# Attention with part of its exponentials on VectorE: one shared factor for the shifted terms, GpSimd adds of two of them, eight key tiles instead of five, and order constants by block

## The chip, the cores and the metric

The kernel runs on one core of one Trainium2 chip. The metric is device time in microseconds of one execution, and lower is better. The engines that matter are TensorE (PE in the profile, with its weight loads as PEld), ScalarE (ACT), VectorE (DVE) and GpSimd (POOL). Each has its own queue of instructions and meets the others only through semaphores. SP is the queue that starts most of the DMAs.

## The reference, cut to what matters

The layer normalises the input, runs an attention of 16 heads of width 28 and, beside it, a feed-forward layer with GELU. The output is x + attention * silu(feed-forward).

```python
xn = _layernorm(x)                                  # 2048 x 448
qkv = (xn @ wqkv).reshape(1, 2048, 3, 16, 28) ...   # q, k, v by head
scores = einsum("bhqd,bhkd->bhqk", q, k) * 28**-0.5
p = softmax(scores)                                 # 16 heads x 2048 x 2048
s = einsum("bhqk,bhkd->bhqd", p, v) ... @ wo        # 2048 x 448
h = gelu(xn @ w1 + b1)                              # 2048 x 1792
g = silu(h @ w2 + b2)
out = x + s * g
```

The softmax has 16 x 2048 x 2048 = 67 million exponentials, and they are most of the work of the element-wise engines.

## The kernel before, in words

**Tiling.** The heads go in four groups of four (G = 4), the queries in four chunks of 512 (C = 4). One group and one chunk make a block, so there are NBLK = 16 blocks. A block has 16 key tiles of 128 keys times 4 heads: 64 score tiles of 128 keys x 512 queries, numbered m, MTOT = 1024 in all. In the last block the same tiles are cut by query columns (`pieces`). Scores are computed with keys on the partitions, so a tile of exponentials goes straight into the product with V, which is accumulated in one PSUM bank (`acc`) for the block. A row of V that is constant gives the softmax sum.

**Two ways for an exponential.** Most tiles go through ACT: `p_scores` computes two tiles (or three, where a third PSUM bank is free: `third`, allowed by block by the tuple `R3`) in one row-tiled PE task, `p_exps` evaluates the exponential of the two or three banks in one ACT instruction (line 1407), and the results lie in one of the P slots until `t_pv` (line 1762) multiplies them with V, four heads side by side in four column strips of PE. The others, called late here and in the code, go through DVE in groups of four tiles (one key tile, four heads). Their scores ride in the free rows of the score tasks (`attach`) or go alone (`p_solo`). `p_apass` (line 1625) turns each score bank into a 16-bit integer by one multiply and add; read as bf16, this is a piecewise linear power of two. `p_expq` (line 1684) makes two more copies of the four tiles by adding an integer of the tuple `SH` to it, which shifts the piecewise curve; the weighted sum of the three curves is close to the exponential. The weights (`VC`) are not applied to the tiles but to V: `p_vs` (line 1695) has GpSimd write a scaled copy of the V tile for either shifted term, and the product with V then takes three passes for a late tile, one with V and two with the scaled copies, where an ACT tile takes one.

**Which tiles are late.** `p_late` asks block by block for NQ[b] groups; `pick` takes the next key tile of the list VT = (15, 14, 13, 12, 11), if it lies at least QDIST tiles ahead of the scores, so that a block can have five groups at most (two in the last block, where it takes a pair of key tiles). It goes on only if fewer than ND4 groups are unfinished, the queue of late scores is shorter than LQ and three buffers (units) of 128 x 2048 are free. A unit is held until the product with V has read it.

**What sets the order.** Nothing is scheduled by hand. The builder runs a planner: every step is a generator that offers tasks with an engine, buffers read and written, an expected duration and a priority; `run` keeps a clock for each engine, always takes the task that could start first (within EPS the one with the better priority), writes its instruction into that engine's queue and the waits before it. So the constants (durations, priorities, distances, NQ) decide the order in each queue, and the chip then runs these fixed queues. `port=True` marks tasks on DVE and GpSimd that the planner keeps from overlapping: the shifts of `p_expq`, the squares of q, the multiply at the end of a block. Projections, the feed-forward products, the normalisation by the softmax sum (`p_epi`: SP DMAs, a power on GpSimd of line 1826, a multiply on GpSimd of line 1835) and the output are further generators with due times (`planned`) in units of m. At m = 584 (GM), in block 9, ACT changes to the GELU and back.

Of the kernel before, what the change touches and what calls it, by code (L numbers as in the profile page):

```python
# [8 lines left out]
ALU = mybir.AluOpType  # L9
ET = mybir.EngineType  # L10

PE, ACT, DVE, POOL, SP = ET.PE, ET.Activation, ET.DVE, ET.Pool, 5

S = 2048
D = 448
# [3 lines left out]
G = 4  # L19
C = 4  # L20
# [6 lines left out]
NBLK = G * C  # L27
MTOT = NBLK * T * 4

GM = 584  # L30
NQ = (3, 14, 13, 13, 17, 3, 14, 8, 16, 1, 21, 18, 14, 14, 18, 21)
QLEAD, QDIST = 60, 20
JMAX, DQ, LQ, ND4, LU = 4, 8, 2, 4, 16
PV0, PVC, MP = 12, 3, 0.124
SLACK = 0.413
URG = 10
SP, AHEAD = 5, 101
R3 = (1, 1, 1, 2, 1, 1, 1, 1, 1, 2, 1, 0, 1, 0, 0, 1)
DUE, UR, M0, M2 = 13, 0.922, 59, 978
VT = (15, 14, 13, 12, 11)  # L40
SM_SCALE = DH ** -0.5
LOG2E = 1.4426950408889634
SH = (0, 42, 85)
VC = (1.0, 0.79296875, 0.63671875)
EXP_LC = 1.6446
NS = 5
EXP_OFF = 64.0 / (LOG2E * SM_SCALE)
LN_EPS = 1e-5
KNORM = 2.5
# [9 lines left out]
SBT = [(f // FT, f % FT) for f in range(F0)]  # L59
SEM, OWN = 0.07, 0.03  # L60
SWITCH = 0.1
JOINT = 0.15
EPS = 0.1
PVN = 2
OVERLAP = 0.083
# [28 lines left out]
class _Kernel:  # L94
# [23 lines left out]
    def sb(self, name, shape, dtype=dt.bfloat16):  # L118
        return self.es.enter_context(self.nc.sbuf_tensor(name, shape, dtype))
# [106 lines left out]
        return min(range(len(self.banks)), key=lambda i: (max(self.free_at(i), self.tE[PE]), self.banks[i][1] in third), default=None)  # L226

    def settle(self):
        again = True
        while again:  # L230
            again = False
            for p in sorted(self.procs, key=lambda p: (-1 if p[4]() else p[0], p[1])):
                op = p[3]
                if isinstance(op, _Task):
                    continue
                if op[0] == "until" and op[1]():
                    self.advance(p)
                    again = True

    def run(self):  # L240
        idle = 0
# [50 lines left out]

    def due(self, *key):
        m = self.plan[key]
        return lambda: 5 if self.in_gelu() else 1.1 if self.next_m > m else SP

    def planned(self):
        K = self
# [46 lines left out]
    def alloc(self):  # L345
# [28 lines left out]
        self.ones = sb("ones", [128, 1], bf)  # L374
        self.csq = sb("csq", [128, G], bf)
        self.colK = sb("colK", [128, G], f32)
        self.vs = sb("vs", [128, 2, NS, 2, 4, 32], bf)
        self.coff = sb("coff", [128, 1], f32)
        self.b2b = self.wv[:, 0, 0:D]
        self.st6 = sb("st6", [128, T, 6], f32)  # L380
# [105 lines left out]
    def schedule(self):  # L486
# [33 lines left out]
        K.late_left = [0] * (NBLK + 3)  # L520
        K.vt = [list(VT) for g in range(G)]
        K.late_on = False
        assert all(len(x) <= NS for x in K.vt)
        K.PB, K.PPREV, K.plast = {}, {}, {}
        K.free_u = []
        K.a_left = {}
        K.h3_free = False
        K.pend_q = []
        K.copying = False
        K.ln2e = 0  # L530
        K.late_blk = 0
        K.banks += [(K.ring[:, b, :], K.b_ring[b]) for b in (3, 2)]
# [561 lines left out]

    def p_q(self, g, c):
        K = self
        bank, tok = yield ("bank", lambda: K.pe_free() and K.ready(K.b_xnT[c] + [K.b_wqk[0][g], K.b_colK, K.b_kT[0][3]]) and ((g, c) == (0, 1) or K.boot()), 1.5 if g == 0 else K.due("kq", g, c))
        K.pe_wait += 1
        for k in range(KT):
            yield K.t_proj(0, g, c, bank, tok, k, 1.5 if g == 0 else K.due("kq", g, c))  # L1100
        K.pe_wait -= 1
        qb = K.qT[:, g, c * 512:(c + 1) * 512]
        qr = _Buf()
        yield _Task(DVE, lambda eng: eng.tensor_copy(qb, bank), [tok], [qr], 0.7, 0.0, 2)  # L1104
        K.banks.append((bank, tok))
        yield ("until", lambda: len(K.qsqs) > 0 if g == 0 else (K.qn_done >= g - 1 and (g > 1 or K.q0_done == 3)))
        i = K.qsqs.pop(0) if g == 0 else c
        qs, tq = K.qsq[:, i, :], K.b_qsq[i]
        if g:
            yield _Task(POOL, lambda eng: eng.tensor_tensor(qs, qb, qb, ALU.mult), [qr], [tq], 1.1, 0.05, 2, port=True)  # L1110
        else:
            yield _Task(DVE, lambda eng: eng.tensor_tensor(qs, qb, qb, ALU.mult), [qr], [tq], 0.43, 0.0, 2, port=True)
        if g:
            K.qn[g].append(qr)
            return
        bank2, tok2 = yield ("bank", lambda: K.ready([tq]), 1.5)
        yield _Task(PE, lambda eng: eng.matmul(bank2, K.bsel[:, :], qs, start=True, stop=True),
                    [tq, K.b_bsel], [tok2], 0.216, 0.17, 1.5 if g == 0 else 4)
        K.qsqs.append(i)
        yield _Task(DVE, lambda eng: eng.scalar_tensor_tensor(qb, bank2, K.colK[:, g:g + 1], qb, op0=ALU.add,  # L1120
                                                              op1=ALU.add), [tok2, K.b_colK, qr], [qr, K.b_qT[g][c]], 0.75, 0.0, 2)
        K.banks.append((bank2, tok2))
        K.q0_done += 1

# [242 lines left out]
    def p_scores(self):  # L1367
        K = self
        u = 0
        while K.next_m < MTOT:  # L1370
            yield ("until", lambda: K.exp_u >= u - 2)
            if K.next_m >= MTOT:
                break
            if K.gu is not None and u == K.gu + 1:
                yield ("until", lambda: K.dir_read == ND)
            b0 = 4 * (u % 2)
            n = 2
            ms = []
            while len(ms) < n and K.next_m < MTOT:
                ms.append(K.next_m)  # L1380
                K.step()
            if K.gu is None and ms[-1] >= GM:
                K.gu = u
            at = {m: K.ring[:, b0 + k, :] for k, m in enumerate(ms)}
            toks = [K.b_ring[b0 + k] for k in range(len(ms))]
            K.pend = p = {"task": K.t_score(ms, at, toks, 1), "ms": ms, "at": at, "toks": toks, "rs": [], "b0": b0}
            yield p["task"]
            K.pend = None
            for (m0, u0, m), x in p["rs"]:
                K.spawn(K.p_apass(u0, m0, m - m0, *x), m0)  # L1390
            K.sc_u = u
            u += 1
# [99 lines left out]

    def pick(self, b):
        K = self
        for t in VT:
            m0 = 64 * b + (4 * t if b < NBLK - 1 else 2 * t - 2)
            if m0 % 4 or m0 in K.late or (b == NBLK - 1 and t - 1 not in VT):
                continue
            if m0 < K.next_m + QDIST:
                return None  # L1500
            K.late |= set(range(m0, m0 + 4))
            K.late_left[b] += 1
            K.nq += 1
            return m0
        return None
# [162 lines left out]
    def p_expq(self, m0, u):  # L1668
        K = self
        b = K.sub_of(m0)  # L1670
        yield ("until", lambda: K.ln2e == 0 and K.a_left[m0] == 0 and K.unit_of(b, 2 if not any(K.sub_of(x) < b for x in K.pend_q) else 4) is not None)
        K.ln2e = 1
        K.need -= 1
        K.pend_q.remove(m0)
        us = [u]
        for _ in range(2):
            v = K.unit_of(b)
            K.free_u.remove(v)
            us.append(v)
        u16 = dt.uint16  # L1680
        bT = K.b_U[u]
        for i in (1, 2):
            W, T, bW = *K.pair(us[i], u), K.b_U[us[i]]
            yield _Task(DVE, lambda eng, W=W, T=T, i=i: eng.tensor_scalar(W.bitcast(u16), T.bitcast(u16), float(SH[i]), None, op0=ALU.add),
                        bT, bW, 0.69, 0.0, 4, port=True)
        K.ln2e = 0
        K.late_ready.append((m0, tuple(us)))

    def p_vs(self, g):
        K = self  # L1690
        yield ("until", lambda: all(K.b_v[1 if g else 0][t].tw is not None for t in K.vt[g]) and (g < 2 or K.E_done >= C * (g - 2) + C - 1))
        for i, t in enumerate(K.vt[g]):
            for v in (1, 2):
                dst, src = K.vs[:, g % 2, i, v - 1, :, :], K.vaug[:, t, 4 * g:4 * g + 4, :]
                yield _Task(POOL, lambda eng, dst=dst, src=src, v=v: eng.tensor_scalar(dst, src, VC[v], 1.0, op0=ALU.mult, op1=ALU.mult),  # L1695
                            [K.b_v[1 if g else 0][t], K.b_vpad, K.b_vpad0], [K.b_vs[g % 2][i]], 0.36, 0.05, 2, port=True)

    def p_pv(self):
        K = self
# [4 lines left out]
        for q in range(0, MTOT // 4, 2):  # L1704
# [2 lines left out]
            b = first  # L1707
            mine = lambda: [x for x in K.late_ready if K.sub_of(x[0]) == b]
            go = lambda: K.exp_m >= ms[-1] and K.E_done >= first - 1
            low = lambda: q % 16 > 0 and K.E_done >= first - 1 and len(K.free_u) < LU and any(K.ready(K.b_U[x[1][-1]]) for x in mine())  # L1710
            while not go():
                yield ("until", lambda: go() or low())
                if not go():
# [1 line left out]
            while end and len(mine()) < K.late_left[b]:  # L1715
                yield ("until", lambda: len(mine()) == K.late_left[b] or (len(K.free_u) < LU and len(mine()) > 0))
                if len(mine()) < K.late_left[b]:
                    yield from self.pv_task(q, mine()[:1], [])
            late = [x for x in K.late_ready if K.sub_of(x[0]) == b and (end or K.ready(K.b_U[x[1][-1]]))]
            yield from self.pv_task(q, late, ms)  # L1720
            for m in ms:
                K.pv_done[m] = True
# [5 lines left out]
    def pv_task(self, q, late, ms):  # L1728
# [4 lines left out]
        K.late_left[b] -= len(late)  # L1733
        src = [(m,) + K.p_slot(m) + (0,) for m in ms if m not in K.late]
        for m0, us in late:
            for v, u in enumerate(us):
                src += [(m0 + k, K.part(u, k), K.b_U[u][k], v) for k in range(4)]
        for i in range(0, len(src), 4 * PVN):
            yield self.t_pv(q, src[i:i + 4 * PVN])
        for _, us in late:  # L1740
            K.free_u += us

    def t_pv(self, q, src):
        K = self
# [2 lines left out]
        for kk in range(4):  # L1747
            for m, ap, tok, v in src:
# [7 lines left out]
                K.pv_begun.add((K.sub_of(m), j))  # L1756

                i = K.vt[g].index(t) if v else 0
                w = K.vs[:, g % 2, i, v - 1, j, :] if v else K.vaug[:, t, 4 * g + j, :]

                def f(eng, j=j, q0=q0, nq=nq, col=col, ap=ap, first=first, w=w, t=t):
                    return eng.matmul(K.acc[32 * j:32 * j + 32, q0:q0 + nq], w,  # L1762
# [176 lines left out]
```

## Time and profile before

| | |
|---|---|
| median of 3 runs | 426.99 us (426.97 to 427.0) |
| profiled execution, its own time | 426.28 us |
| its span, first to last instruction | 424.0 us |
| ACT busy | 404.2 us in 414 instructions |
| PE busy | 402.6 us |
| DVE busy | 339.1 us in 585 instructions |
| GpSimd busy | 146.6 us in 159 instructions |
| first exponential starts | 14.0 us |

The span of the profiled execution is 2.3 us shorter than its own time, and that time 0.7 us shorter than the median. In the profile an instruction's record lasts from its start until its result is written, so records of one engine in a row overlap a little, and "busy" counts the overlap once. A PE that is busy by the records also counts the changes between its tilings, because the modelled end of a matmul reaches over them.

### The profile page before, as it was taken

The numbers are of one execution on the slowest core, as the hardware profiler recorded it, in microseconds if no ns is written. First come the engines' busy times: TensorE is split into PE (matmuls) and PEld (weight loads), VectorE is DVE, ScalarE is ACT, GpSimd is POOL, SyncE is SP. The second block draws the span as 40 slices with busy tenths as digits, with TensorE's granted clock in tenths as the row PEclk, the third lists the DMA queues.
The fourth block names the chain that finished last, engine by engine and source line by source line (L and its number), as shares of the span: only waits on it lengthen the run. The fifth ranks groups of instructions, "written<-read, shape, count | busy, mean of one in ns | idle before, by whom it ended". The sixth has DMA issues, their size and how long they took to land.

```text
span 424.0 us, 9666 instructions
## 1 busy us (share of the span) xinstructions
PE 402.6 (95%) x3708; PEld 136.8 (32%) x3735; DVE 339.1 (80%) x585; ACT 404.2 (95%) x414; POOL 146.6 (35%) x159
## 2 busy tenths in 40 slices
PE   6999999999999999999999999999999999999993
PEld 4443223332222222222223433332232223223551
DVE  7969999999698899996782132187999998999675
ACT  5899999999999999999999999999999999999990
POOL 6583032316351413222223210075083217421512
PEclk9999999999999999999999999999999999999999
DMA  8801010101010100000500100001000000002335
GB/s 265 305 2 39 2 27 2 28 2 36 6 26 2 27 2 23 6 3 27 152 27 5 24 1 2 2 2 29 2 26 2 10 20 21 7 3 57 60 72 88
DMA packets 15368, 15.30 MB, mean 36 GB/s; under 512 B 7037, under 2 KB 12393, under 8 KB 15274
## 3 DMA queue, kind: packets, MB, share of 16 engines
q1 hardware_dynamic: 14170, 12.61, 10.5%
q0 software_dynamic: 864, 1.38, 2.6%
q8 instruction: 30, 0.49, 0.5%
q10 hardware_dynamic: 288, 0.69, 0.4%
q14 instruction: 16, 0.13, 0.1%
HBM read 12.60 MB, written 3.40 MB: 38 GB/s over the span
## 4 chain that ended last, share of the span: by engine, by line
PE 59%; ACT 17%; issue 10%; DVE 7%; POOL 5%; POOLq 0%; ACTq 0%; DVEq 0%
PE ring L1354 18%; PE acc L1762 14%; ACT P L1407 10%; PE ring L1216 7%; ACT h L1407 7%; PE ring L1285 3%; PE misc L862 3%; PE ring L862 2%; PE misc L1285 2%; PE misc L1216 2%; POOL rc L1826 1%; PE acc L1004 1%; PE misc L1155 1%; PE misc L1845 1%; POOL h L1306 1%
## 5 line engine op out<-in xcount | busy, mean ns | idle before, releaser
L1407 ACT ACTIVATE P<-ring 128x1024 bf16<-128x1024 f32 (+1 forms) x248 | 260.7, 1171 | 2.4 <-PE ring L1354 1.8
L1354 PE MATMUL ring<-qT,kT 32*128 32x512 bf16 (+2 forms) x1072 | 143.7, 358 | 5.6 <-ACT h L1407 1.2
L1407 ACT ACTIVATE h<-ring 128x1024 bf16<-128x1024 f32 (+1 forms) x80 | 85.9, 1177 | 0.0
L1354 PEld LDWEIGHTS ring<-qT,kT 32*128 32x128 bf16 x1072 | 38.5, 91 | 139.9 <-ACT P L1407 78.4
L1826 POOL TENSOR_TENSOR rc<-rs,mone 128x16 f32<-128x16 bf16 x15 | 44.5, 2966 | 88.9 <-DMA rs<-sums 88.9
L1762 PE MATMUL acc<-P,vaug 128*32 128x512 bf16 (+2 forms) x638 | 52.6, 352 | 0.3 <-ACT P L1407 0.2
L1216 PE MATMUL ring<-xnT,w 128*128 128x512 bf16 x156 | 41.9, 382 | 1.0 <-issue 1.0
L1407 ACT ACTIVATE xnT<-ring 128x1024 bf16<-128x1024 f32 (+1 forms) x33 | 35.0, 1117 | 0.4 <-PE ring L1354 0.3
L1625 DVE TENSOR_SCALAR x_sb<-ring 128x512 uint16<-128x512 f32 x48 | 32.5, 685 | 3.5 <-PE ring L1354 3.3
L1835 POOL TENSOR_TENSOR qT<-x_sb,E_sb 128x512 bf16<-128x512 f32 x15 | 18.8, 1255 | 47.3 <-DMA x_sb<-recs 37.6
L1110 POOL TENSOR_TENSOR qsq<-qT 128x512 bf16<-128x512 bf16 x12 | 12.8, 1070 | 56.7 <-DVE qT L1104 40.5
L1285 PE MATMUL ring<-w,h 128*128 128x448 bf16 x126 | 30.2, 355 | 0.3 <-DVE qT L1104 0.3
L1354 PE MATMUL misc<-qT,kT 32*128 32x512 bf16 (+1 forms) x80 | 29.6, 376 | 0.0
L1625 DVE TENSOR_SCALAR h<-ring 128x512 uint16<-128x512 f32 x37 | 25.2, 686 | 2.1 <-PE ring L1354 1.2
L1762 PE MATMUL acc<-h,vaug 128*32 128x512 bf16 x220 | 26.2, 384 | 0.0
L1306 POOL TENSOR_TENSOR h<-w 128x448 bf16<-128x448 bf16 x12 | 13.6, 1134 | 35.3 <-ACT w L1301 34.7
L1285 PE MATMUL misc<-w,h 128*128 128x448 bf16 x98 | 25.1, 356 | 0.5 <-DVE w L1291 0.4
L1216 PEld LDWEIGHTS ring<-xnT,w 128*128 128x128 bf16 x164 | 13.8, 97 | 21.3 <-issue 6.5
L1695 POOL TENSOR_SCALAR vs<-vaug 128x128 bf16<-128x128 bf16 x40 | 14.5, 362 | 17.3 <-PE acc L1762 9.3
L1762 PEld LDWEIGHTS acc<-P,vaug 128*32 128x32 bf16 x638 | 13.8, 95 | 15.2 <-issue 11.4
L1291 DVE TENSOR_TENSOR w<-misc,wv 128x448 bf16<-128x448 f32 x7 | 4.3, 620 | 17.2 <-PE misc L1285 17.2
L1216 PE MATMUL misc<-xnT,w 128*128 128x512 bf16 x56 | 17.2, 384 | 0.5 <-issue 0.5
(251 smaller groups left out, 653.2 us busy)
## 6 DMA issues: line engine op xcount, KB each, us to landing
x_sb<-recs SPq DMA_DIRECT2D x60, 64.0 KB, 2.0
w<-in_B_w_dram SPq DMA_DIRECT2D x1, 1568.0 KB, 7.3
w<-in_B_w_dram SPq DMA_DIRECT2D x1, 1344.0 KB, 8.2
out_dram<-in_A_x_dram SPq DMA_DIRECT2D x3, 448.0 KB, 10.7
out_dram<-h POOLq DMA_DIRECT2D x6, 224.0 KB, 4.0
x_sb<-in_A_x_dram SPq DMA_DIRECT2D x2, 448.0 KB, 5.3
h<-in_A_wqkv_dram SPq DMA_DIRECT2D x3, 168.0 KB, 5.1
x_sb<-in_A_x_dram ACTq DMA_DIRECT2D x1, 448.0 KB, 4.3
```

What stands on the lines that cost most here:

```text
L862: return eng.matmul(bank, w[:, k, g * 128:(g + 1) * 128], K.xnT[:, k, c * 512:(c + 1) * 512], start=(k == 0), stop=(k == KT - 1))
L1110: yield _Task(POOL, lambda eng: eng.tensor_tensor(qs, qb, qb, ALU.mult), [qr], [tq], 1.1, 0.05, 2, port=True)
L1216: return eng.matmul(bank, K.w1[:, k, ft * 128:(ft + 1) * 128], K.xnT[:, k, c * 512:(c + 1) * 512], start=(k == 0), stop=(k == KT - 1))
L1285: ins = eng.matmul(ps, hv[:, ft, t * 128:(t + 1) * 128], K.w2[:, ft, :], start=(ft == 0), stop=(ft == FT - 1))
L1306: yield _Task(POOL, lambda eng, o=o, t=t: eng.tensor_tensor(o, sg[:, t, :], fb[:, t, :], ALU.mult), [K.b_sig[c % 2], K.b_fsb[c % 2]], [K.b ...
L1354: return eng.matmul(dst, K.kT[32 * j:32 * j + 32, g, t * 128:(t + 1) * 128], K.qT[32 * j:32 * j + 32, g, c * 512 + q0:c * 512 + q0 + nq], ...
L1407: return eng.activation(reg[:, i0:i0 + n, :], K.ring[:, b0:b0 + n, :], ACTF.Exp, scale=SM_SCALE)
L1625: yield _Task(DVE, lambda eng: eng.tensor_scalar(K.part(u, k).bitcast(dt.uint16), K.like(u, bank), SM_SCALE * LOG2E * 128.0, (127.0 - EXP_ ...
L1695: yield _Task(POOL, lambda eng, dst=dst, src=src, v=v: eng.tensor_scalar(dst, src, VC[v], 1.0, op0=ALU.mult, op1=ALU.mult), [K.b_v[1 if g ...
L1762: return eng.matmul(K.acc[32 * j:32 * j + 32, q0:q0 + nq], w, ap[:, col:col + nq] if len(ap.shape) == 2 else ap[:, col // 128:(col + nq) / ...
L1826: yield _Task(POOL, lambda eng: eng.tensor_tensor(K.rc[:, :], K.rs[:, :], K.mone[:, 0:1].to_broadcast([128, 16]), ALU.pow), [K.b_srs, K.b_ ...
L1835: yield _Task(POOL, lambda eng: eng.tensor_tensor(dst, K.rb, E, ALU.mult), [K.b_rb, tE], [K.b_onT[g][c]], 1.15, 0.05, 1, port=True)
```

## The change: what it does

- **One factor.** `SH` and the constant of the first pass change, and both shifted terms now have the same weight, VC = 0.6875. There is one scaled copy of V a key tile instead of two.
- **Adds on GpSimd.** With one weight the two shifted terms can be added before the product. In blocks whose constant MG is 1, when the scores are more than GE tiles from the end of the group's block and GpSimd's planned queue ends within GQ us, `p_expq` has GpSimd add the third term into the second, in four adds of 128 x 512; one unit becomes free at once and the product takes two passes instead of three. By the change's own words that is a third of the groups.
- **Eight key tiles.** VT has eight entries, and the cap of a block is eight groups (four in the last). NQ changes with it, and `R3`.
- **Constants by block.** The table BP has a row of 18 constants for each block; `tune` puts a row into force when the scores enter the block.
- **Smaller edits.** The first projection of q of the second chunk gets better priorities (Q1, QP); `settle` goes over the waiting generators in another order; readiness of a group looks at all its buffers; the variable SP that stood for two things is split.

```diff
+BPN = ('MG', 'GQ', 'GE', 'EPS', 'PV0', 'PVC', 'MP', 'ND4', 'LU', 'JOINT', 'LQ', 'JMAX', 'DQ', 'URG', 'SLACK', 'UR', 'QLEAD', 'QDIST')
+BP = (
+    (1, 4.0, 12, 0.1, 12, 3, 0.124, 4, 16, 0.15, 2, 4, 8, 8, 0.413, 0.922, -1, 20),
+    (0, 4.0, 12, 0.1, 12, 3, 0.124, 4, 16, 0.116, 2, 4, 8, 8, 0.413, 0.922, 60, 20),
...
+    (1, 4.0, 12, 0.1, 12, 3, 0.124, 4, 16, 0.15, 2, 4, 8, 10, 0.413, 0.922, 60, 20),
+)
-NQ = (3, 14, 13, 13, 17, 3, 14, 8, 16, 1, 21, 18, 14, 14, 18, 21)
+NQ = (3, 13, 13, 13, 14, 5, 15, 8, 16, 4, 16, 16, 12, 14, 15, 16)
...
-R3 = (1, 1, 1, 2, 1, 1, 1, 1, 1, 2, 1, 0, 1, 0, 0, 1)
+MG, GQ, GE = 1, 4.0, 12
+GP, MP4 = 4.2, 1
+R3 = (1, 0, 1, 2, 1, 1, 0, 2, 1, 0, 1, 0, 0, 1, 0, 1)
-VT = (15, 14, 13, 12, 11)
+VT = (15, 14, 13, 12, 11, 10, 9, 8)
-SH = (0, 42, 85)
-VC = (1.0, 0.79296875, 0.63671875)
-EXP_LC = 1.6446
-NS = 5
+SH = (0, 40, 82)
+VC = 0.6875
+EXP_LC = 1.60626
+NS = 8
...
     def settle(self):
-        again = True
-        while again:
-            again = False
-            for p in sorted(self.procs, key=lambda p: (-1 if p[4]() else p[0], p[1])):
...
+        while True:
+            on = [p for p in self.procs if not isinstance(p[3], _Task) and p[3][0] == "until" and p[3][1]()]
+            if not on:
+                return
+            for p in sorted(on, key=lambda p: (-1 if p[4]() else p[0], p[1])):
+                if p[3][1]():
                     self.advance(p)
...
+    def tune(self, b):
+        if BP:
+            globals().update(zip(BPN, BP[b]))
...
     def p_q(self, g, c):
+        dp = Q1 if (g, c) == (0, 1) else 2
+        pp = QP if (g, c) == (0, 1) else 1.5
...
     def p_scores(self):
...
+            if K.next_m // 64 != K.blk:
+                K.blk = K.next_m // 64
+                K.tune(K.blk)
...
     def p_expq(self, m0, u):
...
-        K.late_ready.append((m0, tuple(us)))
+        if MG and K.next_m < 64 * (m0 // 64 + 1) - GE and K.tE[POOL] < K.now + GQ:
+            v, w = us[1:]
+            for k in range(0, 4, MP4):
...
+                    W, X = K.part(v, k), K.part(w, k)
...
+                bs = K.b_U[v][k:k + MP4], K.b_U[w][k:k + MP4]
+                yield _Task(POOL, lambda eng, W=W, X=X: eng.tensor_tensor(W, W, X, ALU.add), bs[0] + bs[1], bs[0], GP * MP4 / 4, 0.05, 2, port=True)
+            K.free_u.append(w)
+            K.n_mg += 1
+            K.late_ready.append((m0, ((u, 0), (v, 1))))
+            return
+        K.late_ready.append((m0, ((us[0], 0), (us[1], 1), (us[2], 1))))
 
     def p_vs(self, g):
...
-            for v in (1, 2):
-                dst, src = K.vs[:, g % 2, i, v - 1, :, :], K.vaug[:, t, 4 * g:4 * g + 4, :]
+            dst, src = K.vs[:, g % 2, i, :, :], K.vaug[:, t, 4 * g:4 * g + 4, :]
...
     def pv_task(self, q, late, ms):
...
-            for v, u in enumerate(us):
+            for u, v in us:
                 src += [(m0 + k, K.part(u, k), K.b_U[u][k], v) for k in range(4)]
...
     def t_pv(self, q, src):
...
-                w = K.vs[:, g % 2, i, v - 1, j, :] if v else K.vaug[:, t, 4 * g + j, :]
+                w = K.vs[:, g % 2, i, j, :] if v else K.vaug[:, t, 4 * g + j, :]
```

## The prediction, written before the result was known

> **What bounds the kernel now.** I read the span and clock first, then the busy shares, then the groups of ACT by shape and the order of time on ACT, and last the room left on DVE, PE and GpSimd, stretch by stretch.
>
> ```profile
> core 0: 424.0 us, clock 0.998
> PE 402.6 (95%) x3708; PEld 136.8 (32%) x3735; DVE 339.1 (80%) x585; ACT 404.2 (95%) x414; POOL 146.6 (35%) x159
> ```
>
> PE's clock was granted in full, so it is no issue. ACT and PE are both at 95%. Which of them is really full is seen from single instructions. The groups of ACT, shapes kept apart, and then ACT in order of time:
>
> ```profile
> L1407 ACT ACTIVATE P<-ring 128x1024 bf16<-128x1024 f32 x196 | 193.1, 1074 | 2.4 <-PE ring L1354 1.8 <-PE misc L1354 0.4
> L1407 ACT ACTIVATE P<-ring 128x1536 bf16<-128x1536 f32 x51 | 75.5, 1554 | 0.0
> ```
>
> ```profile
> 73.69 3.88 ACT L1407 ACTIVATE h<-ring 128x1024 bf16<-128x1024 f32 x4
> 77.30 1.60 ACT L1407 ACTIVATE P<-ring 128x1536 bf16<-128x1536 f32 x1
> 78.63 2.11 ACT L1407 ACTIVATE h<-ring 128x1024 bf16<-128x1024 f32 x2
> ```
>
> Four two-tile exponentials start within 77.30 - 73.69 = 3.61 us, so ACT's own pace is 0.903 us for two tiles and 1.33 for three; the records are longer because they overlap. All shapes together there are 293 twos, 67 threes and one single: 788 tiles. The missing 236 of 1024 are the 236 first passes of line 1625 on DVE, 59 groups of four. At ACT's pace the exponentials cost 293 x 0.903 + 67 x 1.33 + 0.48 = 354 us. From start to start they take 363.4, so only 9 us of waiting are left in them; GELU, tanh and table loads add some 35, the exponentials begin at 14.0 and end at 412.0. **ACT sets the time**: it falls if fewer tiles go through ACT, by 0.903 us for two, or 1.8 for a group.
>
> What DVE has left, by block (I counted the tiles through ACT to find where the scores of a block begin, and the products with the scaled V between two copies of `acc` for its groups: 2, 3, 4, 5, 3, 3, 5, 4, 3, 1, 4, 5, 5, 5, 5, 2). Columns of the windows: length, DVE busy:
>
> ```profile
> 64.70:87.00 22.30, 21.83 (x38) 1.00 0.06 15
> 130.30:153.90 23.60, 19.13 (x31) 1.00 0.05 13
> 219.90:275.30 55.40, 13.12 (x21) 1.00 0.03 6
> 321.60:342.20 20.60, 20.48 (x34) 1.00 0.07 15
> ```
>
> These are blocks 2, 5, 9 and 12. Blocks 2 and 12 are full, 5 has 4.5 us free, 9 (with the GELU) has 42. Likewise blocks 4, 8, 10 and 15 have 3.7, 5.4, 4.1 and 6.4 free. DVE's pace and PE's tasks in order of time:
>
> ```profile
> 61.53 0.69 DVE L1625 TENSOR_SCALAR x_sb<-ring 128x512 uint16<-128x512 f32 x1
> 62.14 0.68 DVE L1684 TENSOR_SCALAR w<-x_sb 128x2048 uint16<-128x2048 uint16 x1
> 62.74 0.69 DVE L1684 TENSOR_SCALAR h<-x_sb 128x2048 uint16<-128x2048 uint16 x1
> 63.34 0.69 DVE L872 CAST kT<-ring 128x512 bf16<-128x512 f32 x1
> ```
>
> ```profile
> 52.25 0.39 PE L1354 MATMUL ring<-qT,kT 32*128 32x512 bf16 x3 [0.15 <-DVE x_sb L1625]
> 52.58 0.40 PE L1762 MATMUL acc<-P,vaug 128*32 128x512 bf16 x4
> 52.80 0.39 PE L1762 MATMUL acc<-h,vaug 128*32 128x512 bf16 x4
> 53.12 0.39 PE L1354 MATMUL ring<-qT,kT 32*128 32x512 bf16 x2
> ```
>
> ```profile
> 150.00:180.00 30.00, 29.11 (x252) 8.23 (x248) 28.88 (x48) 29.97 (x32) 6.87 (x4) 1.00 0.04 11
> ```
>
> A pass or a shift takes 0.60 us from start to start, a group 6 x 0.60 = 3.6 us of DVE. On PE a pass over four strips takes 0.22 and a change between scores and products about 0.1 more (0.33 and 0.32 instead of 0.22). The second fence is a window of all engines (PE, PEld, DVE, ACT, POOL): PE idles 0.9 of 30 us. Over the twelve such windows from 30 to 390 us PE idles 9.9 us. So ACT is first, PE close behind, DVE full in half of the blocks, GpSimd free.
>
> **The change, part by part.**
>
> *More groups.* The list of five tiles was the limit in blocks 3, 6, 11, 12, 13, 14 and (two) in 15; NQ in 5 and 9. Those limits rise to 8, 4, and 5 and 4. Elsewhere buffers and DVE's room set the number. With 3.6 us a group, DVE's room allows one more in 4, 5, 8 and 15 each, and three or more for 9 and 10, whose passes fit into the 42 us; the full blocks get none. That is 7 or 8 by DVE's room; I take 6, because in block 9 PE has no room either (29.3 of 30 us busy at 240 to 270). Ends: 0 (no more than 59 started) and 11. Gain: 6 x 4 tiles / 2 x 0.903 = -10.8 us.
>
> *PE's work for that.* Twelve two-tile rounds fewer save a score pass and two changes each, 12 x 0.42 = -5.0. Six groups need two more passes each: +2.6. A third of 65 groups, 21, is added up by GpSimd and saves a pass: 21 x 0.22 = -4.6. Net -7.0, before the next edit.
>
> *R3.* Three-tile rounds are switched off in blocks 1, 6, 9 and 12, which hold 0, 3, 16 and 2 of the 67, and on in 13. A three does the work of one and a half twos: 21 x (1.5 x 0.903 - 1.33) = +0.5 us on ACT (ends 0, and +1.6 if all 67 go); on PE 10 rounds x 0.42 = +4.4. So PE's work falls by 2.6 us while the time is to fall by some 8; the other 5.7 must come out of the 9.9 us that it idles. It fits, but it is tight, and a rival below.
>
> *Adds.* Nearest row: line 1110, a 128x512 bf16 product on GpSimd, 1.07 us in the mean (1.04 to 1.42). 21 groups x 4 x 1.07 = 90 us more on GpSimd, 237 of some 416: hidden as work. Behind an add stand, in GpSimd's queue, the power and the multiply of a block's normalisation (needed only by the output product much later), and the squares of q for the next head group, which now wait 40 us in all for DVE and not for GpSimd; 4.3 us more delay them little. Without that cover each late square would cost up to 4.3 us at the start of blocks 4, 8 and 12. The products of the group wait for its adds; the GE rule keeps these 12 tiles, some 5 us, from the block's end.
>
> What the adds do to DVE is seen here, a multiply on GpSimd and a shift on DVE:
>
> ```profile
> 292.00 1.22 POOL L1835 TENSOR_TENSOR qT<-x_sb,E_sb 128x512 bf16<-128x512 f32 x1 [1.22 <-DMA x_sb<-recs]
> 292.12 1.65 DVE L1684 TENSOR_SCALAR x_sb<-h 128x2048 uint16<-128x2048 uint16 x1
> ```
>
> The shift starts 0.12 us into the multiply and ends 0.55 after it, instead of after 0.68: it waited out the multiply. Of 118 shifts 13 were stretched so, by 5.5 us in all, against 59 us of such two-input work on GpSimd (lines 1110, 1306, 1308, 1835). 90 us more give 5.5 x 90 / 59 = +8.4 us of DVE. 61% of the groups lie in blocks where DVE has no room, so up to 5.1 reach the path; two banks of scores ahead of ACT take up a part; I take half, **+2.5** (ends 0 and 5.1).
>
> The Trainium skill (SBUF — State Buffer, "Who interferes with whom") states that such a pair of instructions competes for one exclusive pair of ports and that the later one waits for the whole earlier one. The trace agrees for this shift, and by that rule alone, with adds and shifts meeting by chance, the sum would be the third rival's.
>
> *Scaled V.* 32 GpSimd copies of 0.36 us instead of 40: -2.9 us there, all hidden. `SH`, the factor and EXP_LC are numbers in the same instructions: nothing.
>
> *First q projection.* ACT waits at 38.7 and 42.2 us for 0.6 and 0.4 us, about where block 1 begins. Better priority can take both away or delay other copies as much: -0.5 (ends -1.0, +1.0).
>
> *Constants by block, `settle`.* They add no instruction, only order. They could take away at most the 9 us that ACT waits; the worst 30 us window (1.5 us) everywhere would give +10. I take 0, as nothing shows a direction.
>
> Sum against the profiled execution: 426.3 - 10.8 + 0.5 + 2.5 - 0.5 = 418.0; the median lies 0.7 above it: **418.7**, in round numbers 419.
>
> **The rivals.**
> 1. *PE becomes the bound.* For: 0.9 us idle in 30, and the idle lies in pieces between changes. Against: some is waiting for ACT, which shrinks by itself. If PE gives none of it, the time falls by the 2.6 us of its work only: 424.4 in the median; the groups then shorten nothing more.
> 2. *Many more groups.* Eleven fill the caps where DVE is free: -19.9 + 0.5 + 3 - 0.5 = -16.9, 410.1. For: 42 us free in block 9. Against: PE would have to give 12 us, more than it idles; so 412 to 415 rather.
> 3. *Slower: the port.* Adds on GpSimd hold up shifts, DVE runs its queue in order, first passes behind hold PSUM banks, and scores and ACT wait. Place: blocks 1 to 3, 6, 7 and 11 to 14. Price: if 130 shifts met the adds by chance, one in 90 us of some 385 (a share of 0.23), and waited half of 1.07 us, DVE would lose 130 x 0.23 x 0.53 = 16 us; all of it on the path: -10.8 + 0.5 - 0.5 + 16 = +5.2, 432. It decides from the point where two thirds of it (10.8 us) reach ACT. Against: the planner knows the port and only 13 of 118 shifts were hit before. The rule of the Trainium skill named above (SBUF — State Buffer, "Who interferes with whom") speaks for it; this trace shows the wait, but not how often adds would cause it.
> 4. *No more groups.* Buffers or unfinished groups stay the limit, the longer list is not used: the count stays 59, the adds only free PE, ACT's work is what it was: 427 plus or minus 0.8.
>
> **How the numbers follow.** A change under 0.2% (0.85 us) can't be told from none here. Forecast, 416 to 423: 0.47. PE bound, 423 to 426.1: 0.19. Many more groups, 409 to 416: 0.12. Count unchanged, 426.1 to 427.8: 0.06. The port, 427.8 to 434: 0.16. So faster 0.78, same 0.06, slower 0.16. The range leaves out the lower part of the second rival (0.05) and the upper half of the port's (0.09): 411 to 429.
>
> **What would show it.** First passes on line 1625's successor: 4 x 65 = 260 instead of 236, and ACT's twos and threes worth 764 tiles; if they are 236, rival 4. A two-tile pace of still 0.903 us; if ACT's starts lie further apart and PE is the one before each wait, rival 1; if DVE is, rival 3, and then many shifts take over 1 us. GpSimd busy near 235 us with some 84 adds. Products with the scaled V: 8 a group, 4 where added. Most wrong would be the count of groups, which the trace before bounds only by the room on DVE and PE.

## The result: slower, 433.3 us instead of 427.0

The changed kernel takes 433.33 us in the median of four runs (431.71 to 434.28), the kernel before 426.98 us. The ratio is 1.0145, with a 95% interval of 1.0108 to 1.0183. The forecast was 419.0 us, with a range of 411 to 429. The profiled execution of the changed kernel took 434.26 us for a span of 432.4 us, 8.4 us more than the span before. The fences below answer to the ones of the prediction. First the clock and the busy shares after the change:

```profile
core 0: 432.4 us, clock 0.980
PE 409.8 (95%) x3650; PEld 134.6 (31%) x3650; DVE 352.1 (81%) x597; ACT 402.0 (93%) x413; POOL 238.3 (55%) x235
```

ACT has 2 us less work and a lower share, and PE no longer has its full clock. GpSimd rose from 146.6 to 238.3 us; 237 was expected. The largest groups of ACT by shape (busy, mean of one, idle time before them and what ended it):

```profile
L1439 ACT ACTIVATE P<-ring 128x1024 bf16<-128x1024 f32 x211 | 205.9, 1063 | 6.3 <-PE misc L1383 3.9 <-PE ring L1383 1.9
...
L1439 ACT ACTIVATE P<-ring 128x1536 bf16<-128x1536 f32 x39 | 58.5, 1513 | 4.2 <-PE ring L1383 4.0 <-PE misc L1383 0.3
```

Before, these two groups idled 2.4 and 0.0 us; now it is 6.3 and 4.2, and both wait for scores from PE (line 1383, the old 1354). Counted from start to start, with 0.903 us for two tiles and 1.33 for three as in the prediction:

| term | before | after | difference, us |
|---|---|---|---|
| late groups | 59 | 61 | |
| exponentials of two, three, one tile | 293, 67, 1 | 300, 60, 0 | -3.5 |
| waiting of ACT within the exponentials | 9.2 us | 20.3 us | +11.1 |
| last exponential to the end of the span | 12.05 us | 12.9 us | +0.85 |
| sum, to be held against the span's +8.4 | | | +8.45 |

The first row of differences is 7 x 0.903 - 7 x 1.33 - 0.48. So a small gain came in and a larger wait was added. The wait is not spread out: by stretches of 30 us ACT waits 5.7 us from 210 to 240 and 5.7 us from 390 to 420, and at most 1.7 in any other.

**The first place, block 8.** The waits of PE (line, what it waited for, total us, times, longest) show two new ones of nearly the same length, both for an add of line 1729:

```profile
PE acc L1808 <- POOL h L1729: 2.8, 1, 2.8
PE acc L1808 <- POOL vaug L1729: 2.7, 1, 2.7
```

The second is in block 8. GpSimd in order of time (start, length, instruction; idle before it in brackets):

```profile
208.99 1.15 POOL L1729 TENSOR_TENSOR kT<-kT,x_sb 128x512 bf16<-128x512 bf16 x1
213.82 2.91 POOL L1872 TENSOR_TENSOR rc<-rs,mone 128x16 f32<-128x16 bf16 x1 [3.69 <-DMA rs<-sums]
216.70 4.93 POOL L1729 TENSOR_TENSOR vaug<-vaug,x_sb 128x512 bf16<-128x512 bf16 x4
```

The power of the normalisation (line 1872, the old 1826) waits for a DMA, and the four adds of a group stand behind it in GpSimd's queue. Why the DMA is late is seen on SP's queue:

```profile
204.90 0.40 SPq L732 DMA_DIRECT2D w<-in_B_w_dram  x1
206.18 0.53 SPq L1868 DMA_DIRECT2D sums<-E_sb  x1
212.16 0.34 SPq L1870 DMA_DIRECT2D rs<-sums  x1
```

The load of the second feed-forward weight, 1.6 MB, was issued 1.3 us ahead of the small transfer of the softmax sums. The next step, which waits for that transfer, could be issued only 5.98 us after it. The power is late, the adds end at 221.6, and the next task in PE's queue was the products of this group, the added tile among them:

```profile
218.69 0.39 PE L1383 MATMUL ring<-qT,kT 32*128 32x512 bf16 x2
221.77 0.62 PE L1808 MATMUL acc<-kT,vaug 128*32 128x512 bf16 x4 [2.69 <-POOL vaug L1729]
```

The scores behind that product came late by as much, and ACT paused:

```profile
223.40 1.02 ACT L1439 ACTIVATE P<-ring 128x1024 bf16<-128x1024 f32 x1 [3.02 <-PE misc L1383]
224.91 1.02 ACT L1439 ACTIVATE P<-ring 128x1024 bf16<-128x1024 f32 x1 [0.49 <-PE ring L1383]
226.85 1.02 ACT L1439 ACTIVATE P<-ring 128x1024 bf16<-128x1024 f32 x1 [0.91 <-PE misc L1383]
```

After the pause of 3.0 us two smaller ones follow. The windows (length, then PE, PEld, DVE, ACT, POOL busy, granted clock of PE, DMA share, GB/s) show why:

```profile
215.00:220.00 5.00, 3.92 (x29) 0.95 (x26) 4.41 (x6) 5.00 (x6) 5.00 (x4) 1.00 0.04 5
220.00:225.00 5.00, 3.23 (x23) 0.64 (x24) 2.08 (x5) 1.49 (x3) 2.78 (x3) 0.59 0.15 52
225.00:230.00 5.00, 5.00 (x30) 1.30 (x29) 3.74 (x7) 3.79 (x4) 0.00 (x0) 0.72 0.00 0
...
405.00:410.00 5.00, 2.21 (x39) 1.07 (x38) 0.80 (x2) 2.04 (x3) 3.07 (x3) 0.87 0.91 207
410.00:415.00 5.00, 5.00 (x98) 3.02 (x98) 2.83 (x4) 4.24 (x4) 2.02 (x2) 0.50 0.48 71
```

PE stood still until 221.8 us. In the two windows from 220 to 230 us its granted clock was 0.59 and 0.72 in the mean: it was 0.50 from 220.9 to 227.8 us. The matmuls of 0.39 us take 0.6 there, and PE, full at that clock, feeds ACT too slowly.

**The second place, the last block.** GpSimd again, some 190 us later:

```profile
397.80 1.16 POOL L1729 TENSOR_TENSOR h<-h,x_sb 128x512 bf16<-128x512 bf16 x1 [0.74 <-DVE x_sb L1716]
398.91 3.79 POOL L1872 TENSOR_TENSOR rc<-rs,mone 128x16 f32<-128x16 bf16 x1
402.65 1.10 POOL L1908 DMA_DIRECT2D out_dram<-h  x1
403.52 2.52 POOL L1729 TENSOR_TENSOR h<-h,x_sb 128x512 bf16<-128x512 bf16 x2
405.72 1.16 POOL L1908 DMA_DIRECT2D out_dram<-h  x1
406.34 1.73 POOL L1729 TENSOR_TENSOR h<-h,x_sb 128x512 bf16<-128x512 bf16 x1
```

The four adds of one group are pulled apart by a power and by two issues of output DMAs that lie in the same queue. From the first to the last they take 10.3 us, where four in a row take 4.5. PE waits 2.79 us for the last of them, and ACT 2.96 us for PE:

```profile
405.02 0.40 PE L1383 MATMUL ring<-qT,kT 32*128 32x128 bf16 x8
408.21 0.29 PE L1808 MATMUL acc<-x_sb,vaug 128*32 128x256 bf16 x4 [2.79 <-POOL h L1729]
```

```profile
409.45 2.42 ACT L1439 ACTIVATE P<-ring 128x1536 bf16<-128x1536 f32 x2 [2.96 <-PE ring L1383]
```

The clock falls to 0.50 here too, as the last two windows above show.

### The profile page after: what moved, and what is told of

The parts are those of the page before. It is cut to its first block, busy times and chain, and to the rows that moved or that the text cites. A ratio compares the mean times of both kernels' runs of the same rounds, so it can differ in the third digit from the quotient of the medians.

```text
span 432.4 us, 9689 instructions
## 1 busy us (share of the span) xinstructions
PE 409.8 (95%) x3650; PEld 134.6 (31%) x3650; DVE 352.1 (81%) x597; ACT 402.0 (93%) x413; POOL 238.3 (55%) x235
## 4 chain that ended last, share of the span: by engine, by line
PE 67%; DVE 12%; issue 7%; ACT 7%; POOL 5%; POOLq 0%; ACTq 0%; DVEq 0%
PE ring L1383 20%; PE acc L1808 16%; PE ring L1245 9%; ACT P L1439 5%; PE misc L1314 4%; PE ring L1314 3%; PE misc L1245 3%; PE misc L889 2%; PE ring L889 2%; DVE x_sb L1657 2%; PE ring L1184 2%; ACT xnT L1439 2%; PE misc L1184 1%; PE acc L1031 1%; DVE w L1657 1%
## 5 line engine op out<-in xcount | busy, mean ns | idle before, releaser
L1808 PE MATMUL acc<-P,vaug 128*32 128x512 bf16 (+2 forms) x625 | 56.0, 363 | 0.0
L1245 PE MATMUL ring<-xnT,w 128*128 128x512 bf16 x168 | 45.4, 386 | 0.0
L1657 DVE TENSOR_SCALAR x_sb<-ring 128x512 uint16<-128x512 f32 x55 | 37.0, 685 | 7.6 <-PE ring L1383 7.1
L1383 PE MATMUL misc<-qT,kT 32*128 32x512 bf16 (+1 forms) x95 | 35.4, 380 | 0.3 <-DVE kT L1657 0.2
L1314 PE MATMUL misc<-w,h 128*128 128x448 bf16 x112 | 28.6, 356 | 0.5 <-DVE vaug L1657 0.4
L1139 POOL TENSOR_TENSOR qsq<-qT 128x512 bf16<-128x512 bf16 x12 | 12.9, 1072 | 29.5 <-DVE qT L1133 17.9
L1808 PE MATMUL acc<-h,vaug 128*32 128x512 bf16 (+1 forms) x211 | 28.2, 383 | 0.0
L1335 POOL TENSOR_TENSOR h<-w 128x448 bf16<-128x448 bf16 x12 | 14.0, 1164 | 19.0 <-ACT w L1330 12.4
L1729 POOL TENSOR_TENSOR kT<-kT,x_sb 128x512 bf16<-128x512 bf16 x16 | 18.5, 1180 | 10.8 <-DVE x_sb L1716 10.6
L899 DVE CAST kT<-misc 128x512 bf16<-128x512 f32 x9 | 6.2, 686 | 19.2 <-PE misc L889 19.2
L1657 DVE TENSOR_SCALAR x_sb<-misc 128x512 uint16<-128x512 f32 x25 | 17.1, 685 | 3.2 <-PE misc L1383 3.0
L1808 PEld LDWEIGHTS acc<-P,vaug 128*32 128x32 bf16 x625 | 14.5, 98 | 15.8 <-issue 12.5
L1741 POOL TENSOR_SCALAR vs<-vaug 128x128 bf16<-128x128 bf16 x32 | 10.2, 320 | 13.9 <-PE acc L1808 7.4
## 6 DMA issues: line engine op xcount, KB each, us to landing
out_dram<-in_A_x_dram SPq DMA_DIRECT2D x3, 448.0 KB, 11.1
```

The costliest lines, as they stand in the source:

```text
L1245: return eng.matmul(bank, K.w1[:, k, ft * 128:(ft + 1) * 128], K.xnT[:, k, c * 512:(c + 1) * 512], start=(k == 0), stop=(k == KT - 1))
L1314: ins = eng.matmul(ps, hv[:, ft, t * 128:(t + 1) * 128], K.w2[:, ft, :], start=(ft == 0), stop=(ft == FT - 1))
L1335: yield _Task(POOL, lambda eng, o=o, t=t: eng.tensor_tensor(o, sg[:, t, :], fb[:, t, :], ALU.mult), [K.b_sig[c % 2], K.b_fsb[c % 2]], [K.b ...
L1383: return eng.matmul(dst, K.kT[32 * j:32 * j + 32, g, t * 128:(t + 1) * 128], K.qT[32 * j:32 * j + 32, g, c * 512 + q0:c * 512 + q0 + nq], ...
L1657: yield _Task(DVE, lambda eng: eng.tensor_scalar(K.part(u, k).bitcast(dt.uint16), K.like(u, bank), SM_SCALE * LOG2E * 128.0, (127.0 - EXP_ ...
L1729: yield _Task(POOL, lambda eng, W=W, X=X: eng.tensor_tensor(W, W, X, ALU.add), bs[0] + bs[1], bs[0], GP * MP4 / 4, 0.05, 2, port=True)
```

## The experiments

Three accounts could explain the result. By the first (A in the expectations), the place of the adds in GpSimd's queue delays PE at a few points. By the second (B), the order that the constants by block make is worse, whatever the adds cost. By the third (C), the prediction's third rival, adds and shifts hold each other up on the port that GpSimd and DVE share, and the loss is spread. Further questions were the longer list, the constants by block and how near PE is to being the bound. All ratios are against the kernel before, run beside it; all intervals are 95%.

**Adds that cost almost nothing, in the same queues.** Each add works on 4 of its 512 columns, so the output lacks most of the third term in the added tiles.

```diff
-    eng.tensor_tensor(W, W, X, ALU.add)
+    eng.tensor_tensor(W[:, 0:4], W[:, 0:4], X[:, 0:4], ALU.add)
```

> Every add of GpSimd handles 4 of its 512 columns only; all queues, waits and the order of instructions stay as in the changed kernel. It leaves out most of the addition of the two shifted terms. Theory A (the loss is PE waiting for late adds in GpSimd's queue, at two places, 218.7 to 221.8 us and 405.4 to 408.2 us, and what follows them): both waits vanish, ACT's waiting falls from 20.3 us to 9 to 11, time 422 to 425. Theory B (the order that the constants by block make is worse on PE or DVE, whatever the adds cost): 431 to 434. Theory C (adds and shifts hold each other up all over the kernel, the port of my third rival): the same as A here, 422 to 425, with shifts over 0.72 us falling from 17 to 12 or so.

Measured: 424.08 us, ratio 0.9922 (0.9898 to 0.9945); ACT waits 10.7 us, and neither long wait of PE is left. Shifts of over 0.72 us fell from 17 to 10. So the time of the adds is the whole loss and more, and account B, 431 to 434, is out. The power of block 8 is late here too (214.18 us), but the four adds behind it take 0.65 us instead of 4.93 and are done before PE comes for them. This run alone does not part the queue from the port, since short adds relieve both; the next three do.

**The weight load later.** One edit to the point at which the 1.6 MB load is asked for:

```diff
-    yield ("until", lambda: K.next_m >= 64 * 2 * C and all(u in K.free_u for u in (3, 4, 5)))
+    yield ("until", lambda: K.next_m >= 64 * 2 * C + 30 and all(u in K.free_u for u in (3, 4, 5)))
```

> The load of W2 (1.6 MB) is issued 30 tiles of scores later, behind the two small DMAs of the softmax sums of block 7 instead of ahead of them; all other queues are the same. Theory A: the power on GpSimd starts at about 210 us instead of 213.8, the adds behind it end 3 us earlier, ACT's pause of 3.1 us near 220 us and the low clock after it go; time 427.5 to 430, that is 4 to 5 us less. Theory B and theory C: no change, 432 to 434. If the W2 load in its new place delays the second feed-forward product, a new wait of PE near 250 us shows it.

Measured: 429.31 us, ratio 1.0057 (1.0040 to 1.0074), so 0.9% or some 4 us below the changed kernel. SP's queue of this run:

```profile
205.20 0.52 SPq L1868 DMA_DIRECT2D sums<-E_sb  x1
206.84 0.33 SPq L1870 DMA_DIRECT2D rs<-sums  x1
207.35 0.40 SPq L732 DMA_DIRECT2D w<-in_B_w_dram  x1
```

The second step now follows 1.64 us after the first instead of 5.98, and on GpSimd the adds no longer wait for a late power:

```profile
209.12 2.91 POOL L1872 TENSOR_TENSOR rc<-rs,mone 128x16 f32<-128x16 bf16 x1
212.72 4.49 POOL L1729 TENSOR_TENSOR vaug<-vaug,x_sb 128x512 bf16<-128x512 bf16 x4 [0.69 <-DVE x_sb L1716]
```

The pause in block 8 is gone; the one in the last block is left, and ACT waits 14.7 us in all.

**No adds in the last block, and both edits together.** 

```diff
-        if MG and K.next_m < 64 * (m0 // 64 + 1) - GE and ...
+        if MG and m0 < 64 * 15 and K.next_m < 64 * (m0 // 64 + 1) - GE and ...
```

> The two groups of the last block are not added by GpSimd (19 added groups instead of 21); until block 14 the queues are the same. Theory A: PE's wait of 2.8 us at 405.4 us goes, ACT's waiting after 400 us falls from 5.1 to under 1 us, time 427 to 429.5. Theory B: no change, 432 to 434. Theory C: 0.5 us less, 432.5 to 433.5.

> W2 later and no adds in the last block, together. Theory A: both pauses go, 422.5 to 425.5, faster than the kernel before by 0.5% or so, because 8 tiles fewer go through ACT (3.6 us) and ACT's waiting is 10 to 11 us against 9.2. Theory B: 431 to 434. Theory C: 431 to 433; what then remains against the run with thin adds is the price of the port.

Measured: with the last block's adds left out alone, 430.26 us, ratio 1.0075 (1.0052 to 1.0098); the pause in block 8 is as it was, the late one gone. With both edits, 425.46 us, ratio 0.9965 (0.9952 to 0.9978); ACT waits 9.9 us. So the two places cost 0.9% and 0.7%, and together 1.8%, some 8 us: all of the loss. The port account falls with it: with both edits 19 shifts are stretched past 0.72 us, by 10.6 us in all, as in the changed kernel (17, by 10.8), and ACT waits 9.9 us in all, 0.7 more than before the change.

**Only one group of the last block not added.** This asks whether a group of the last block does harm if its adds stay in one piece. With the weight load later:

```diff
-        if MG and K.next_m < ...
+        if MG and m0 != 64 * 15 + 24 and K.next_m < ...
```

> W2 later, and in the last block one of the two groups is added by GpSimd; its four adds now stand in one piece ahead of the power of block 14 and of the output transfers in GpSimd's queue (20 added groups). Theory A1 (adds cost the last block its time only where the power and the output transfers stand ahead of them): no pause of PE over 1 us after 390 us, time 424.5 to 426, like W2 later with no adds in the last block (425.5). Theory A2 (any add in the last block ends too late, because its products are near the end): 427 to 429.5, like W2 later alone (429.3).

Measured: 424.95 us, ratio 0.9952 (0.9937 to 0.9968), the lowest of the kernels that compute everything, and below both kernels. Its GpSimd queue near the end, and its clock in the stretch of the first place:

```profile
389.35 4.49 POOL L1729 TENSOR_TENSOR h<-h,x_sb 128x512 bf16<-128x512 bf16 x4 [6.11 <-DVE x_sb L1716]
393.79 2.91 POOL L1872 TENSOR_TENSOR rc<-rs,mone 128x16 f32<-128x16 bf16 x1
```

```profile
220.00:225.00 5.00, 4.40 (x42) 1.26 (x39) 4.94 (x8) 4.69 (x6) 1.16 (x1) 1.00 0.04 14
```

The adds of the remaining group run in one piece ahead of the power, and the clock stays at 1.00. Against the adds of four columns (0.9922) the whole price of real adds is then about 0.3%, 1.3 us, and the two intervals overlap; what the port costs on the path should lie within that, though the two runs differ in the place of the weight load and of one group's adds as well.

**Five tiles in the list.** Both edits of above, and the list and its scaled copies cut back.

```diff
-VT = (15, 14, 13, 12, 11, 10, 9, 8)
-NS = 8
+VT = (15, 14, 13, 12, 11)
+NS = 5
```

> The run with W2 later and no adds in the last block, but with the list of five key tiles instead of eight, and five scaled copies of V a head group instead of eight. The builder writes the same late groups (2, 3, 5, 4, 4, 3, 4, 4, 4, 4, 4, 5, 5, 3, 5, 2 by block, 61) and the same queues but for 12 copies fewer on GpSimd. Theory D (the longer list is never used, buffers and the queue of late scores set the number): 425.0 to 425.7, no difference. Rival (the eight tiles are what made two more groups possible): 427 to 430.

Measured: 425.44 us, ratio 0.9969 (0.9957 to 0.9982), the same as with eight tiles (0.9965). The count of groups is 61 in both. By block the changed kernel has 2, 3, 5, 4, 4, 3, 4, 4, 4, 4, 4, 5, 5, 3, 5, 2: nowhere more than the five that the old list allowed. Eight tiles change nothing in this order. In other orders they are used: by the products with the scaled V, the run with the table and no adds below has six groups in block 12, and the share alone has three in the last block, where the old list allowed two.

**Adds and constants, each without the other.** All of these have the weight load later. The one called the share alone has neither adds nor the table by block, with the constants of before; the second has adds (none in the last block) and the constants of before; the third the table and no adds. NQ and R3 are those of after in all three. The table also holds MG, which switches the adds off in blocks 1, 3, 6 and 12; without it they are allowed everywhere.

```diff
-        if BP:
+        if False:                    # share alone, and constants off
-        if MG and K.next_m < ...
+        if False and K.next_m < ...  # share alone, and adds off
-QLEAD, QDIST = 0, 12
-JMAX, DQ, LQ, ND4, LU = 2, 3, 2, 3, 3
+QLEAD, QDIST = 60, 20                # share alone, and constants off
+JMAX, DQ, LQ, ND4, LU = 4, 8, 2, 4, 16
...
```

> W2 later, no adds on GpSimd at all, and the order constants of the kernel before in all blocks: what is left of the change is the shared factor, eight key tiles, NQ and R3. 62 late groups, all with three passes. If the constants by block matter little: 62 groups take 12 tiles from ACT against 59, 5.4 us, so 421 to 424. If the order of the queues is worth more than the number of groups: the builder's own clock for this order ends 1.8 us later than for the kernel before, which gives 427 to 430.

> The run with W2 later and no adds in the last block, with the constants by block undone: every block has the order constants of the kernel before. 57 late groups, 24 of them added on GpSimd. By the work alone: 16 tiles more through ACT than with 61 groups, +7.2 us, 432 to 434. If the order counts too (the builder's own clock ends 15 us later than with the constants by block): 438 to 443, with ACT's waiting for PE over 15 us and spread over the kernel.

> The changed kernel with W2 later and no adds at all, constants by block kept: 62 late groups with three passes, an order written anew. By work alone: 4 tiles less through ACT than with 61 groups (-1.8 us), PE 4.6 us more: 423 to 428. If the constants by block fit only the order with adds (the builder's own clock ends 11.6 us later than with W2 later and no adds in the last block): 435 to 439.

| weight load later, ratio to the kernel before | constants of before | constants by block |
|---|---|---|
| no adds | 1.0043 (1.0028 to 1.0058), 62 groups, ACT waits 14.5 us | 1.0210 (1.0194 to 1.0225), 62 groups, 18.9 us |
| adds, none in the last block | 1.0317 (1.0300 to 1.0333), 57 groups, 21.3 us | 0.9965 (0.9952 to 0.9978), 61 groups, 9.9 us |

The three take 428.60, 440.26 and 435.16 us, each within the second range of its expectation: the order counts, and not the work alone. In these runs neither part is good alone. The table is worth 3.5%, 15 us, beside the adds: 16 tiles fewer through ACT (7.2 us) and 11.4 us less waiting, less 4 us after the last exponential. Without the adds it costs 1.7%, 7 us, but one place alone holds 12.4 us of waiting: from 348.7 to 361.7 us PE takes 68 products of line 1314 (the second feed-forward layer) with no scores between them, and ACT stands 6.2 us before a tanh and another 6.2 us after it. The second of these is not in the 18.9 us, which counts from an exponential to the next instruction of ACT. In the run with adds and old constants the waits of ACT name products, not adds:

```profile
ACT P L1439 <- PE acc L1808: 4.6, 2, 3.4
ACT xnT L1439 <- PE acc L1808: 4.6, 1, 4.6
```

PE has other work ahead of the scores at those points, and the longest wait of PE for an add is 1.2 us; the order is bad, and no single late add is to blame.

**The weight load later, in the kernel before.** A control: the same edit where no adds stand behind the power.

> The kernel before, with the W2 load issued 30 tiles later and nothing else changed. Theory A: no adds stand behind the power on GpSimd there, so its late sums cost nothing: 426.5 to 427.3, no difference. Rival (the W2 load itself disturbs PE or the transfers of either kernel): 2 to 4 us less, as in the changed kernel.

Measured: 426.29 us, ratio 1.0005 (0.9993 to 1.0018). The power moves from 210.98 to 206.17 us:

```profile
206.17 2.91 POOL L1826 TENSOR_TENSOR rc<-rs,mone 128x16 f32<-128x16 bf16 x1 [2.81 <-DMA rs<-sums]
```

and ACT's waiting stays as it was (9.15 us for 9.24). The late power was there all along, and harmless until products depended on what is queued behind it.

**How near PE is to being the bound.** The version with one group less added, and the added tile of each of its 20 groups multiplied a second time, with the planner told the old duration, so that the queues keep their order. The output then counts that term twice.

```diff
-            K.late_ready.append((m0, ((u, 0), (v, 1))))
+            K.late_ready.append((m0, ((u, 0), (v, 3))))   # t_pv issues the products of kind 3 twice
```

> The run with W2 later and one added group in the last block; the added tile is multiplied with the scaled V twice (so its term counts double), which gives PE back the third pass that the adds save: 20 groups x 0.22 = 4.4 us, in the same queues. If PE is as full as ACT: 428.5 to 430. If PE has room where the products stand: 425 to 426.

Measured: 426.82 us, ratio 1.0012 (1.0000 to 1.0024), against 0.9952 without the second products: 0.6%, 2.6 us, for 20 x 0.22 = 4.4 us of PE work. ACT waits 12.6 instead of 10.6 us. About 60% of it reaches the end (40 to 80% by the two intervals), between the two expectations: PE is neither the bound nor free.

**A nudge of the planner.** As the version with one group less added, with the expected duration of a first pass 0.695 instead of 0.69 us.

```diff
-            [tok], [K.b_U[u][k]], 0.69, 0.0, 1)
+            [tok], [K.b_U[u][k]], 0.695, 0.0, 1)
```

> The run with W2 later and one added group in the last block; the builder is told 0.695 us for a first pass on DVE instead of 0.69, nothing else. It writes another order with 59 late groups, 25 of them added, and its own clock ends 27 us later. Theory E (the builder's choices are so sensitive that the number of groups and the time are mostly a matter of which order it falls into, and the chip follows its clock): 440 to 454. Rival (on the chip such differences wash out, since the instructions are the same in kind and nearly in number): 427 to 431.

Measured: 455 to 460 us, ratio 1.0730 (1.0672 to 1.0789), more than either expectation. A number that no instruction carries, changed by 0.7%, takes the order to 59 groups and makes the kernel 7% slower than the one before. The constants by block fit the one order that they were made beside; in the two other orders that were run with them (this one and the one without adds) the kernel is slower than the one before.

## Why the prediction was wrong

The prediction's sum was -10.8 + 0.5 + 2.5 - 0.5 = -8.3 us; in the same terms the profile gives +8.45.

- **"More groups", "I take 6": wrong by size.** There are 2 more, and with the rounds of three, ACT's work fell by 3.5 us instead of 10.3. This is 6.8 us of the error. The step read the list of five tiles as the limit in seven blocks; cutting the list back to five changed nothing in this order, and the blocks 3, 6 and 13 fell from five groups to four, four and three with eight tiles to choose from. The gain that it counted on in block 9 came (four groups for one). By the conditions in `p_late` the free buffers, the queue of late scores and the distance end a block earlier; that is argued from the code, and no run varied them singly. The range given for it, 0 to 11 groups, held the value.
- **"Hidden as work", wrong by mechanism.** The work of the adds was sized well: 84 of them, 1.15 us each by the record for an expected 1.07, GpSimd 238 us for 237. What was queued behind the adds was looked at, but not what the adds themselves would be queued behind. They stand behind a power that waits for a DMA and behind output DMAs, and the products that need them hold PE's queue and so the scores. The step said that the GE rule keeps the products' wait away; it keeps some 5 us of distance in planned time, and the planner knew neither the weight load ahead of the sums nor the DMA issues on GpSimd. Measured: +11.1 us of waiting and +0.85 at the end, 9.95 us more than the +2.5 and the -0.5 of the prediction; undoing both places gives 1.8% back.
- **The port, right in kind and not on the path.** The shifts lost 5.1 us more than before (10.8 for 5.7 by the same count; the prediction has 5.5); expected were 8.4 on DVE, of which 2.5 on the path. With the two places mended the stretching is the same and ACT waits 9.9 us for the 9.2 of before. By the rule of the Trainium skill (SBUF — State Buffer, "Who interferes with whom") the later instruction of such a pair waits for the whole earlier one; the trace agrees, with a shift of 1.52 us beside the adds at 217.98 us instead of 0.68. The third rival's time, 432, was near the result, but its mechanism was not what cost it.
- **"Constants by block: I take 0", wrong.** The step bounded them by the 9 us that ACT waited in the kernel before and by its worst window. But with adds and the old constants (and NQ and R3 of after) ACT waits 21.3 us and has 16 tiles more, so the constants are worth 15 us beside the adds, beyond the 9 us that the step allowed. The baseline of that term was the wrong one: it held the constants against the work of the kernel before, and took them as order alone, while they also decide how many groups become late.
- **PE close behind, right.** Added PE work reaches the time by about 60%. The first rival as such (PE gives none of its idle time) did not come about: ACT's pace of 0.903 us stands, and the long waits are single events.
- **First q projection, right in sign:** up to 50 us ACT's waiting fell from 1.60 to 0.66 us, -0.9 for an expected -0.5; no run varied the projection alone. The scaled copies of V cost nothing, as said.

What one profile can't settle: with the two places mended, the terms give -3.5 + 1.4 + 1.6 = -0.5 us for the best version (ACT waits 10.6 us, and 13.7 us follow the last exponential), while the medians differ by 2.0. Its profiled execution lies 0.6 us above its median, that of the kernel before 0.7 below; the rest stays open.

## What to carry to other kernels

Free time on an engine is not a free place in its queue: before work on which others wait is moved there, list what stands ahead of it and what that waits for, DMAs on other queues included. A late instruction that harms nobody becomes a stall once something needed stands behind it. And where a planner writes the order, a part can't be priced against the old constants: price the part with its own order, and look first for what the planner's clock does not know.

## What the runs showed of the hardware

- With a standstill of PE of 2.7 to 2.8 us its granted clock went to 0.50 for 6.8 us, at both places (220.9 to 227.8 and 408.7 to 415.5 us; the windows of 5 us above mix this with the full clock). In the versions without these waits the windows there show 1.00. The Trainium skill (TensorE: Matmul & The Clock Gate, "What's actually happening") puts the fall at an idle window of about 3.4 us; here less was enough, though PE was nearly full before (4.76 of 5 us busy from 210 to 215). Such a standstill is not the only way to a lower clock: in the run of the share alone it was 0.50 for 3.4 us from 196.3 us on, with no wait of PE over 0.45 us in the 8 us before. Why is not shown.
- A small transfer issued 1.3 us behind a 1.6 MB load on SP's queue took until 5.98 us after its issue before its successor went out, 1.64 us without the load ahead (in the kernel before, with the load 0.9 us ahead, 6.29 us, and 1.64 with the load later).
- On GpSimd an issue of an output DMA held its queue for 0.86 to 1.16 us, and the power that takes 2.9 us otherwise took 3.79 in the last block.
- The same 128x512 bf16 shape takes 1.15 us on GpSimd as an add of two tiles and 1.04 (in the median) as a square, which reads one tile twice.
